# All four pairs of heads mixed in one step, values and plain-path loads taken two pairs at a time, in an attention + ELU + SiLU kernel

## The chip, the core and the metric

The kernel runs on one core of one Trainium2 chip. The metric is device time in microseconds (us) of one launch on that core; the lower the better. The median of the kernel before is 925.0 us, of three runs from 924.09 to 925.73 us. "p", "scores" and the like are named as in the code; TensorE is PE in the rows, VectorE DVE, ScalarE ACT, GpSimd POOL, SyncE SP.

## The reference

Causal attention with a window of 128 keys and a linear bias per head, then two feed-forward layers with weights of 512 x 2048 and 2048 x 512; everything is float32.

```python
def _attn_ref(q, k, v):                      # q, k, v: (4, 8, 576, 64)
    scores = scale * np.matmul(q, k.transpose(0, 1, 3, 2))
    mask = (rel >= 0) & (rel < window)       # rel: query position less key position, window 128
    scores = np.where(mask, scores + bias[None], -1000000000.0)
    scores = scores - np.max(scores, axis=-1, keepdims=True)
    attn = np.exp(scores)
    attn = attn / (np.sum(attn, axis=-1, keepdims=True) + 1e-09)
    return np.matmul(attn, v)

x = attn_out.transpose(0, 2, 1, 3).reshape(2304, 512)
h = x @ w_in
x = np.where(h > 0.0, h, np.exp(np.minimum(h, 0.0)) - 1.0) @ w_out
h = x @ w2_in
out = (h * (1.0 / (1.0 + np.exp(-h)))) @ w2_out
```

## The kernel before

The 2304 tokens are 18 groups of 128. **Attention** runs over 36 *units*: unit `u` is a pair of groups `t = u // 4` and a pair of heads `hp = u % 4`. In the loop over `u` these steps follow each other, each for a unit of its own age, and on every engine instructions run in the order in which the loop writes them (the schedule is by hand):

- `scores(u)`: PE computes the scores of both heads (`s`), DVE adds the bias and takes the row maxima (line 512, four instructions a unit), ACT takes the four exponentials (line 517). Units below `PLAIN` = 16 multiply plain float32 (line 495); later ones multiply operands split in a rounded upper part and a remainder (line 498).
- `invert(u - 1)`, `normal(u - 1)`: DVE inverts the sums (lines 520, 521), POOL scales p (line 560).
- `turn(u - 2)`: PE transposes p (line 536); `evict(0)` on DVE and `evict(1)` on ACT copy it to `ptt` in SBUF (lines 547, 549).
- `mix(u - 4)`, in units of even number: PE multiplies values and transposed p of two units, that is of two pairs of heads, into `a` (line 579), and `keep` on ACT writes the result to `store[0][block]` (line 585), the input x of the first layer. Values are loaded for one pair of heads at a time (`load_v`).

The first layer's work fills PE's time between those steps. Groups of tokens form five *blocks* (of 2, 4, 4, 4, 4 groups). When the last pair of a block's last groups has been mixed, the block's x is complete. Then `split_x(block, c)` splits each of the four 128-row chunks c of x in `xh` (ACT, line 227) and `xl` (DVE, line 228), and the block's pieces go to the list `fill`: for every slice of the hidden layer four pieces `c = 0..3` of three matmuls (`h`, line 244), later the pieces of the second product (`y`, line 302). `point(n)` takes pieces from the head of that list, for four token groups `n` of them, at three points of a unit, `PIECES = (2, 1, 2)`: two behind `scores(u)`, one behind `mix`, two at the end of the unit. `may` stops the list at its head while a piece's operands aren't known to have been written.

The first two pairs' chunks c = 0, 1 are split two units before chunks 2, 3, since the first `mix` of a group pair stands in unit 4t + 4 and the second in unit 4t + 6:

```python
keep = mix(u - 4)                      # u even
...
if o + 2 * P == blocks[bi][1] * P:     # the block's last groups
    split_x(bi, hp - 1)
    split_x(bi, hp)
```

SP issues nearly all loads. In attention it loads per unit the keys (`load_k`), the queries (`load_q`) and the values; ten slices of weights of the first layer are loaded in units 1 to 14 (`WSLOTS`), and go through POOL, ACT and DVE (`rescale`, `sign`, `join`, `part`: lines 142 to 167) before PE can use them. The last block and everything behind it, both layers, run after attention in `layers`: `h` and `y` matmuls without a break.

Of the kernel before, what the change touches and what calls it, by code (L numbers as in the profile page):

```python
# [42 lines left out]
def attention_elu_silu_kernel(  # L43
# [40 lines left out]
    LAG = 2  # L84
    NR = 4
    PLAIN = 16
    WSLOTS = [*range(1, 15), *range(26, 34)]
    PIECES = (2, 1, 2)
    BANKS = 3
    UNITS = [(t, hp) for t in range(NG // 2) for hp in range(NPAIR)]  # L90
# [238 lines left out]
    def attention():  # L329

        with ExitStack() as actx:
# [12 lines left out]

            kk = [const.tile([P, 2, 2, 3 * P], F32R, tag=f"k{hp}", name=f"k{hp}") for hp in range(NPAIR)]

            vv = [[const.tile([P, 2, P], F32, tag=f"v{hp}{i}", name=f"v{hp}{i}") for i in range(2)]
                  for hp in range(NPAIR)]
            raw_k, raw_q, qs, lows, lows_k = {}, {}, {}, {}, {}

            def first_col(g):
# [9 lines left out]
                for j in range(2):  # L361
                    eng.memset(qz[(1 - j) * D:(2 - j) * D, i, j, :], 0.0)

            def load_k(u, eng=nc.sync):
                if u < NU:
                    t, hp = UNITS[u]
                    c0 = first_col(2 * t)
                    if u < PLAIN:
                        eng.dma_start(kz[:, u % 4, c0:], k[hp * P:(hp + 1) * P, (2 * t - 1) * P + c0:2 * (t + 1) * P])
                        return  # L370
                    if t == PLAIN // NPAIR:
                        r = kw[:, u % 2, 0:6 * P].rearrange("p (j t) -> p j t", j=2)
# [9 lines left out]
            def load_q(u, eng=nc.sync):  # L382
                if u < NU:
                    t, hp = UNITS[u]
                    if u < PLAIN:
                        for j in range(2):
                            eng.dma_start(qz[j * D:(j + 1) * D, u % 4, j, :],
                                          q[hp * P + j * D:hp * P + (j + 1) * D, 2 * t * P:2 * (t + 1) * P])
                        return
                    raw_q[u] = r = r_p.tile([P, 2, 2 * P], F32, tag="kqr", name="qr")  # L390
                    for x in range(2):
                        eng.dma_start(
                            r[x * D:(x + 1) * D],
                            q[hp * P:(hp + 1) * P, 2 * t * P:2 * (t + 1) * P].rearrange("(j d) t -> d j t", d=D))

            def load_v(u):
                if u < NU:
                    t, hp = UNITS[u]
                    nc.sync.dma_start(
                        vv[hp][t % 2],  # L400
                        v[2 * t * P:2 * (t + 1) * P, hp * P:(hp + 1) * P].rearrange("(g p) d -> p g d", p=P))

            clear(0)
            load_q(0, nc.scalar)
            load_k(0)
# [5 lines left out]
            load_k(1)  # L411
            load_q(1)
            ident = const.tile([P, P], F32, tag="ident", name="ident")
            make_identity(nc, ident)
            ident16 = const.tile([P, P], BF16, tag="ident16", name="ident16")
# [105 lines left out]
                nc.vector.reciprocal(sums[u], sums[u])  # L521

            pts = {}

            def turn(u):
                t, hp = UNITS[u]
                pt = ps_.pop(u)
                ptt = pts[u] = pt_p.tile([P, 2, 4 * P], F32, tag="ptt", name="ptt")
                ev = []
                for j in range(2):  # L530
                    ps = ps_t.tile([P, 4 * P], F32, tag="t", name="pt")
                    parts = []
                    for e in range(2):
                        c0 = first_col(2 * t + e)
                        for c in range(c0, 2 * P, P):
                            nc.tensor.transpose(ps[:, 2 * P * e + c:2 * P * e + c + P], pt[:, j, e, c:c + P], ident)  # L536
                        if parts and c0 == 0:
# [12 lines left out]
                return evict  # L550
# [11 lines left out]
            def mix(u):  # L562

                t, hp = UNITS[u]
                bi, o = home[2 * t]
                ps = ps_a.tile([P, 2, 2 * P], F32, tag="a", name="a")
                c0 = first_col(2 * t)

                parts = [(2 * t, 1, 3), (2 * t + 1, 3, 4)]
# [4 lines left out]
                for i in range(2):  # L574
                    ptt = pts.pop(u + i)
                    for x, (g, a, b2) in enumerate(parts):
                        q0, q1 = (a // 2) * P, ((b2 + 1) // 2) * P
                        for j in range(2):
                            nc.tensor.matmul(ps[j * D:(j + 1) * D, i, q0:q1],  # L579
                                             vv[hp + i][(g // 2) % 2][:, g % 2, j * D:(j + 1) * D],  # L580
                                             ptt[:, j, a * P:b2 * P], start=(i == 0 and x == 0),
                                             stop=(i == 1 and x == len(parts) - 1), skip_group_check=True)

# [5 lines left out]

            fill, fresh, rest = [], [], []  # L590
            known = set()
            held = [0]

            def group(made, freeing, cost, ready):
# [43 lines left out]
            for u in range(NU + 3):  # L638
# [1 line left out]
                calls[0] += 1  # L640
                last = 2 * FIRST_F + (u >= 20) * NRAW
                if u in WSLOTS:
                    weight_step(min(u + 2, last), (4, 1), 1, last)
                pop()
                if u < NU:
                    scores(u)
                point(PIECES[0])
                low_q(u + 1)
                low_k(u + 1)
                while owed:  # L650
                    owed.pop(0)()
                if u in WSLOTS:
                    weight_step(min(u + 2, last), (2, 3), 1, last)
# [36 lines left out]
                if u < 2:  # L690
# [119 lines left out]
```

## Time and profile before

| | |
|---|---|
| median of three runs | 925.0 us (924.09 to 925.73) |
| the profiled execution, its own time | 923.84 us |
| its span, first to last instruction | 922.1 us |
| granted TensorE clock, mean | 1.000 |
| PE busy | 909.5 us, 99% |
| DVE, ACT, POOL busy | 571.2, 434.4, 229.4 us |
| DMA | 59.82 MB, mean 65 GB/s |

The profiled execution took 1.74 us more than its span, and lies 1.2 us below the median. PE is busy nearly all the time, so the time is PE's own work plus the moments in which it waits. DVE, ACT and POOL are far from full over the whole span, but not in the first 60 us.

### The profile page before, as it was taken

Reading aid. Unit: us, or ns where it says so; the run is one execution under the profiler, and the core shown is the slowest. Engines: PE = TensorE matmul, PEld = TensorE weight load, DVE = VectorE, ACT = ScalarE, POOL = GpSimd, SP = SyncE. Lnnn points to the kernel's source line nnn. Section 1 sums busy time; section 2 is a strip of 40 time slices with the busy share of each in tenths; the row PEclk is TensorE's granted clock in tenths of the full one; section 3 lists DMA queues with packets and bytes.
Section 4 is the critical chain, followed back from the end, with each engine's and each line's share of the span. In section 5 each row is a group of like instructions: output and inputs, shape, how many; then the busy total and the mean of one; then the engine's idle time right before and its main releaser. Section 6 shows DMA issues by size and latency. Waiting matters only on the chain.

```text
span 922.1 us, 13077 instructions
## 1 busy us (share of the span) xinstructions
PE 909.5 (99%) x4754; PEld 761.0 (83%) x4754; DVE 571.2 (62%) x1186; ACT 434.4 (47%) x959; POOL 229.4 (25%) x316
## 2 busy tenths in 40 slices
PE   7999999999999999999999999999999999999998
PEld 5878888887878888889888888888888888888887
DVE  7996878983778776576555546644366554444422
ACT  7786777764555435333343255543533342233311
POOL 5544455553444202220012023220221021000000
PEclk9999999999999999999999999999999999999999
DMA  8634336320242202210002012210221010000011
GB/s 250 206 99 109 97 107 176 94 68 6 90 134 91 69 1 70 69 46 1 1 13 79 23 46 71 73 41 24 68 69 47 1 46 1 34 35 23 23 46 45
DMA packets 50479, 59.82 MB, mean 65 GB/s; under 512 B 3952, under 2 KB 44144, under 8 KB 50416
## 3 DMA queue, kind: packets, MB, share of 16 engines
q1 hardware_dynamic: 50256, 58.87, 21.0%
q8 instruction: 37, 0.61, 0.3%
q14 instruction: 26, 0.21, 0.1%
q10 hardware_dynamic: 160, 0.13, 0.1%
HBM read 54.26 MB, written 4.72 MB: 64 GB/s over the span
## 4 chain that ended last, share of the span: by engine, by line
PE 89%; DVE 3%; issue 3%; POOL 2%; DMA 1%; ACT 1%; SPq 0%; POOLq 0%; DVEq 0%; ACTq 0%
PE y L302 40%; PE h L244 39%; PE a L579 3%; PE pt L536 3%; PE s L495 2%; PE s L498 2%; POOL wl L164 1%; POOL wraw L142 1%; DMA y<-in_k_dram 1%; DVE p L512 1%; DVE gl L272 0%; DMA v<-in_v_dram 0%; DMA wraw<-in_moe_w_in_dram 0%; DVE e L257 0%; DVE k L465 0%
## 5 line engine op out<-in xcount | busy, mean ns | idle before, releaser
L244 PE MATMUL h<-xh,wh 128*128 128x512 f32 (+1 forms) x640 | 238.5, 373 | 0.0
L244 PE MATMUL h<-xl,wh 128*128 128x512 f32 (+1 forms) x640 | 235.7, 368 | 0.6 <-DVE xl L228 0.6
L244 PE MATMUL h<-xh,wl 128*128 128x512 f32 (+1 forms) x640 | 235.7, 368 | 0.0
L164 POOL TENSOR_TENSOR wl<-wraw,wh 128x512 fp32r<-128x512 f32 x54 | 75.5, 1401 | 401.4 <-ACT wh L162 401.4
L272 DVE TENSOR_TENSOR gl<-e,gh 128x512 fp32r<-128x512 f32 (+1 forms) x158 | 106.0, 671 | 103.8 <-ACT gh L266 103.6
L251 ACT ACTIVATE e<-h 128x512 f32<-128x512 f32 (+1 forms) x160 | 88.1, 551 | 173.6 <-PE h L244 152.7
L266 ACT ACTIVATE gh<-e 128x512 fp32r<-128x512 f32 (+1 forms) x160 | 94.0, 588 | 106.6 <-DVE e L258 63.8
L244 PEld LDWEIGHTS h<-xh,wh 128*128 128x128 f32 x640 | 120.7, 189 | 20.4 <-issue 1.2
L244 PEld LDWEIGHTS h<-xh,wl 128*128 128x128 f32 x640 | 120.6, 188 | 20.3
L244 PEld LDWEIGHTS h<-xl,wh 128*128 128x128 f32 x640 | 120.7, 189 | 19.9 <-DVE xl L228 0.8
L302 PE MATMUL y<-gh,wh 128*128 128x512 f32 (+1 forms) x320 | 121.1, 379 | 0.0
L302 PE MATMUL y<-gl,wh 128*128 128x512 f32 (+1 forms) x320 | 118.3, 370 | 0.9 <-DVE gl L272 0.8
L302 PE MATMUL y<-gh,wl 128*128 128x512 f32 (+1 forms) x320 | 117.9, 368 | 0.0
L302 PE MATMUL y<-wl,gh 128*128 128x512 f32 (+1 forms) x294 | 113.1, 385 | 0.0
L302 PE MATMUL y<-wh,gh 128*128 128x512 f32 (+1 forms) x294 | 113.1, 385 | 0.0
L302 PE MATMUL y<-wh,gl 128*128 128x512 f32 (+1 forms) x294 | 113.1, 385 | 0.0
L560 POOL TENSOR_SCALAR p<-p,sm 128x256 f32<-128x256 f32 (+2 forms) x144 | 72.6, 521 | 98.8 <-DVE sm L521 52.6
L260 DVE TENSOR_TENSOR e<-h,e 128x512 f32<-128x512 f32 (+1 forms) x80 | 51.0, 638 | 60.4 <-ACT e L251 59.7
L162 ACT ACTIVATE wh<-wraw 128x512 fp32r<-128x512 f32 x58 | 38.5, 667 | 90.9 <-DVE wraw L154 66.7
L517 ACT ACTIVATE p<-p,neg 128x256 f32<-128x256 f32 (+2 forms) x144 | 68.9, 481 | 19.9 <-DVE neg L512 18.3
L302 PEld LDWEIGHTS y<-gl,wh 128*128 128x128 f32 x320 | 60.4, 189 | 11.3 <-DVE gl L272 2.2
L302 PEld LDWEIGHTS y<-gh,wh 128*128 128x128 f32 x320 | 60.3, 189 | 11.0 <-issue 1.0
(76 smaller groups left out, 1194.7 us busy)
## 6 DMA issues: line engine op xcount, KB each, us to landing
wraw<-in_moe_w_in_dram SPq DMA_DIRECT2D x30, 512.0 KB, 3.8
wraw<-in_moe_w_out_dram SPq DMA_DIRECT2D x28, 512.0 KB, 3.3
qr<-in_q_dram SPq DMA_DIRECT2D x40, 128.0 KB, 2.9
v<-in_v_dram SPq DMA_DIRECT2D x36, 128.0 KB, 2.6
out_dram<-x SPq DMA_DIRECT2D x17, 256.0 KB, 2.0
kr<-in_k_dram SPq DMA_DIRECT2D x32, 128.0 KB, 2.9
y<-in_k_dram SPq DMA_DIRECT2D x12, 192.0 KB, 3.7
y<-in_q_dram SPq DMA_DIRECT2D x30, 64.0 KB, 2.9
```

Of the source, the lines that this page charges most:

```text
L162: nc.scalar.activation(h, f32(top), AF.Copy)
L164: nc.gpsimd.tensor_tensor(lo, f32(top), f32(h), op=ALU.subtract)
L244: nc.tensor.matmul(tiles["ps"][:, 0:w], a[:, cs], b2[:, c, 0:w], start=(c == 0 and x == 0), stop=(c == NKC - 1 and x == 2))
L251: nc.scalar.activation(e[:, 0:w], tiles["ps"][:, 0:w], AF.Exp if layer == 0 else AF.Sigmoid)
L260: nc.vector.tensor_tensor(e[:, 0:w], ps[:, 0:w], e[:, 0:w], op=ALU.mult)
L266: nc.scalar.activation(gh[:, 0:w], tiles["e"][:, 0:w], AF.Copy)
L272: eng.tensor_tensor(gl[:, 0:w], tiles["e"][:, 0:w], f32(gh[:, 0:w]), op=ALU.subtract)
L302: nc.tensor.matmul(tiles["ps"][:, s], a[:, cs], b2[:, s], start=(f == f0 and x == 0), stop=(f == f1 - 1 and x == 2))
L517: nc.scalar.activation(dst, dst, AF.Exp, bias=m, scale=-1.0, accum_out=a)
L536: nc.tensor.transpose(ps[:, 2 * P * e + c:2 * P * e + c + P], pt[:, j, e, c:c + P], ident)
L560: nc.gpsimd.tensor_scalar(dst, dst, by, 1.0, op0=ALU.mult, op1=ALU.mult)
L579: nc.tensor.matmul(ps[j * D:(j + 1) * D, i, q0:q1], vv[hp + i][(g // 2) % 2][:, g % 2, j * D:(j + 1) * D], ptt[:, j, a * P:b2 * P], start= ...
```

## The change

In units with `u % 4 == 2` two mixes stand one behind the other, `mix(u - 6)` and `mix(u - 4)`, and units with `u % 4 == 0` have none; only the last group pair keeps the old places (units 36 and 38). So that transposed p of the first two pairs can wait longer, its `ptt` lies in places of `store` that are not in use yet (`homes`). The first of the two mixes takes a PSUM buffer of the transposes (`ps_t`). A block's x is then complete all at once: chunks 0 and 1 are split at the end of that unit, chunks 2 and 3 in the next unit behind `scores(u)`, and pieces c = 2, 3 may not be taken before that has been written. Values are loaded for two pairs of heads at a time; keys and queries of the plain units, from unit 2 on, as well. Weights are loaded one unit later than before, from unit 0 on, and wait one more unit until they are rescaled, so that `rescale`, `sign`, `join` and `part` of the ten slices stay in their units.

```diff
-    WSLOTS = [*range(1, 15), *range(26, 34)]
+    WSLOTS = [*range(15), *range(26, 34)]
...
-            def load_k(u, eng=nc.sync):
+            def load_k(u, eng=nc.sync, n=2):
...
-                        eng.dma_start(kz[:, u % 4, c0:], k[hp * P:(hp + 1) * P, (2 * t - 1) * P + c0:2 * (t + 1) * P])
+                        if u % n == 0:
+                            eng.dma_start(
+                                kz[:, u % 4:u % 4 + n, c0:],
+                                k[hp * P:(hp + n) * P, (2 * t - 1) * P + c0:2 * (t + 1) * P].rearrange("(h p) t -> p h t", p=P))
...
             def load_v(u):
-                if u < NU:
+                if 0 <= u < NU and u % 2 == 0:
                     t, hp = UNITS[u]
                     nc.sync.dma_start(
-                        vv[hp][t % 2],
-                        v[2 * t * P:2 * (t + 1) * P, hp * P:(hp + 1) * P].rearrange("(g p) d -> p g d", p=P))
+                        vv[hp // 2][t % 2],
+                        v[2 * t * P:2 * (t + 1) * P, hp * P:(hp + 2) * P].rearrange("(g p) d -> p g d", p=P))
...
-                ptt = pts[u] = pt_p.tile([P, 2, 4 * P], F32, tag="ptt", name="ptt")
+                if t < NG // 2 - 1 and hp < 2:
+
+                    ptt = homes[min(t, 4)][:, hp].rearrange("p (j t) -> p j t", j=2)
+                else:
+                    ptt = pt_p.tile([P, 2, 4 * P], F32, tag="ptt", name="ptt")
+                pts[u] = ptt
...
                 if u in WSLOTS:
-                    weight_step(min(u + 2, last), (4, 1), 1, last)
+                    weight_step(min(u + 1, last), (4, 1), 2, last)
                 pop()
                 if u < NU:
                     scores(u)
                 point(PIECES[0])
                 low_q(u + 1)
+                while later:
+                    bi = later.pop()
+                    split_x(bi, 2)
+                    split_x(bi, 3)
                 low_k(u + 1)
...
                 if u % 2 == 0 and u >= 4:
-                    keep = mix(u - 4)
+
+                    if u - 4 >= NU - NPAIR:
+                        keep = mix(u - 4, ps_a)
+                    elif u % NPAIR == 2:
+                        mix(u - 6, ps_t)()
+                        keep = mix(u - 4, ps_a)
                 point(PIECES[1])
-                load_v(u)
+                load_v(u - 2)
...
-                        split_x(bi, hp - 1)
-                        split_x(bi, hp)
+                        if t < NG // 2 - 1:
+                            split_x(bi, 0)
+                            split_x(bi, 1)
+                            later.append(bi)
+                        else:
+                            split_x(bi, hp - 1)
+                            split_x(bi, hp)
...
-                                made_ready += [group(hidden(bi, f), 1, n, lambda i, f=f: (0, 0, f) in known)] * NKC
+                                made_ready += [group(hidden(bi, f), 1, n, lambda i, f=f, bi=bi: (0, 0, f) in known and (i < 2 or bi not in later))] * NKC
```

On ACT, around the end of unit 22 and in unit 23 (x of block 2 is `x_78`, complete in unit 22), the order before is:

```order
L517 ACTIVATE p,sm<-p,neg 128x256 x4
L310 ACTIVATE y_82<-y 128x512
L585 ACTIVATE x_78<-a 128x2x256
L310 ACTIVATE y_82<-y 128x512
L549 ACTIVATE ptt<-pt 128x512
L227 ACTIVATE xh<-x_78 128x512 x2
L472 ACTIVATE qs<-qr 128x512
L517 ACTIVATE p,sm<-p,neg 128x256 x4
L310 ACTIVATE y_82<-y 128x512
L549 ACTIVATE ptt<-pt 128x512
```

and of the changed kernel at the same place:

```order
L523 ACTIVATE p,sm<-p,neg 128x256 x4
L310 ACTIVATE y_82<-y 128x512
L601 ACTIVATE x_78<-a 128x2x256 x2
L310 ACTIVATE y_82<-y 128x512
L562 ACTIVATE y_84<-pt 128x512
L227 ACTIVATE xh<-x_78 128x512 x2
L478 ACTIVATE qs<-qr 128x512
L523 ACTIVATE p,sm<-p,neg 128x256 x4
L227 ACTIVATE xh<-x_78 128x512 x2
L310 ACTIVATE y_82<-y 128x512
L562 ACTIVATE y_84<-pt 128x512
```

Before, the pair of `xh` here is that of chunks 2 and 3, with chunks 0 and 1 two units back; now it is that of chunks 0 and 1, and the pair of chunks 2 and 3 stands behind the four exponentials of unit 23. On DVE the two `xl` of chunks 2 and 3 move in the same way, behind the row maxima of unit 23 and `qs`.

PE's own order in unit 23 stays as it is: `scores(23)`, the fill pieces c = 0 and c = 1 (three rows `h` each), piece c = 2, then the transposes of unit 21; likewise in units 15 and 31.

On PE in unit 24, where a mix of two pairs stands between the fill pieces before (`a` rows), the order before is

```order
L244 MATMUL h<-xh,wl_572 128x512
L579 MATMUL a<-ptt,v_123 64x256 x2
L579 MATMUL a<-ptt,v_123 64x128 x2
L579 MATMUL a<-ptt,v_122 64x128 x2
L579 MATMUL a<-ptt,v_125 64x256 x2
L579 MATMUL a<-ptt,v_125 64x128 x2
L579 MATMUL a<-ptt,v_124 64x128 x2
L244 MATMUL h<-xh,wh_571 128x512
```

and now

```order
L244 MATMUL h<-xh,wl_341 128x512
L244 MATMUL h<-xh,wh_340 128x512
L244 MATMUL h<-xl,wh_340 128x512
L244 MATMUL h<-xh,wl_341 128x512
L549 MATMUL pt<-ident,p 128x128 x8
```

The `a` rows are gone from between the fill pieces; twice as many stand behind each other in unit 26. In the whole program eight such places are gone (units 4, 8, ..., 32), five of them (16 to 32) between fill pieces of 128 x 512.

## Rows read from the trace of the kernel before

**Rows 1.** The page: engines' busy time, and the chain that ended last by engine.

```profile
PE 909.5 (99%) x4754; PEld 761.0 (83%) x4754; DVE 571.2 (62%) x1186; ACT 434.4 (47%) x959; POOL 229.4 (25%) x316
...
PE 89%; DVE 3%; issue 3%; POOL 2%; DMA 1%; ACT 1%; SPq 0%; POOLq 0%; DVEq 0%; ACTq 0%
```

**Rows 2.** Busy time by stage: from:to, length, engines' busy us, clock, DMA.

```profile
0.00:20.00 20.00, 13.99 (x71) 10.33 (x72) 13.96 (x65) 13.84 (x47) 10.91 (x31) 1.00 0.83 240
20.00:40.00 20.00, 18.55 (x128) 15.27 (x128) 19.69 (x65) 17.73 (x54) 11.01 (x20) 1.00 0.80 244
40.00:60.00 20.00, 18.95 (x139) 15.23 (x136) 18.16 (x63) 14.93 (x44) 7.84 (x15) 1.00 0.35 93
...
80.00:220.00 140.00, 139.56 (x947) 115.70 (x946) 115.09 (x339) 96.53 (x272) 73.35 (x126) 1.00 0.36 100
```

**Rows 3.** Timeline of unit 23: start, duration, engine, line; in brackets idle before.

```profile
126.46 1.14 ACT L227 ACTIVATE xh<-x 128x512 fp32r<-128x512 f32 x2
127.08 1.12 PE L498 MATMUL s<-k,qs 128*128 128x256 f32 x8
127.11 1.71 DVE L228 TENSOR_TENSOR xl<-x,xh 128x512 fp32r<-128x512 f32 x2 [0.95 <-ACT xh L227]
...
129.42 0.39 PE L244 MATMUL h<-xh,wh 128*128 128x512 f32 x1
...
130.11 1.04 PE L536 MATMUL pt<-ident,p 128*128 128x128 f32 x8
...
131.15 0.19 ACT L517 ACTIVATION_READ_ACCUMULATOR p<-p,neg 128x1 f32 x1
```

**Rows 4.** Timeline of unit 31, in the same columns.

```profile
179.38 1.28 DVE L228 TENSOR_TENSOR xl<-x,xh 128x512 fp32r<-128x512 f32 x2
...
181.28 0.39 PE L244 MATMUL h<-xh,wh 128*128 128x512 f32 x1
...
181.97 1.04 PE L536 MATMUL pt<-ident,p 128*128 128x128 f32 x8
...
182.83 0.19 ACT L517 ACTIVATION_READ_ACCUMULATOR p<-p,neg 128x1 f32 x1
```

**Rows 5.** Timeline of unit 15.

```profile
79.93 0.39 PE L244 MATMUL h<-xh,wh 128*128 128x512 f32 x1
80.01 0.19 ACT L517 ACTIVATION_READ_ACCUMULATOR p<-p,neg 128x1 f32 x1
...
80.62 1.04 PE L536 MATMUL pt<-ident,p 128*128 128x128 f32 x8
```

**Rows 6.** Timeline of PE in unit 32: a mix between fill pieces.

```profile
186.35 0.39 PE L244 MATMUL h<-xh,wl 128*128 128x512 f32 x1
186.66 1.96 PE L579 MATMUL a<-ptt,v 128*64 128x256 f32 x24
188.55 0.50 PE L244 MATMUL h<-xh,wh 128*128 128x512 f32 x1
188.89 0.40 PE L244 MATMUL h<-xl,wh 128*128 128x512 f32 x1
```

**Rows 7.** Timeline of the first 18 us: PE, ACT and DVE.

```profile
3.50 6.88 PE L495 MATMUL s<-y,y 128*128 128x128 f32 x24 [3.50 <-DVE bias L431]
...
11.59 0.68 ACT L144 ACTIVATE wraw<-wraw 128x512 int32<-128x512 uint32 x1 [1.53 <-DMA wraw<-in_moe_w_in_dram]
...
12.01 1.48 PE L495 MATMUL s<-y,y 128*128 128x128 f32 x8
...
16.36 1.97 PE L495 MATMUL s<-y,y 128*128 128x256 f32 x8 [1.30 <-DMA y<-in_k_dram]
...
17.61 0.42 DVE L512 CUSTOM_DVE_ANT_0 p<-s,bias 128x256 f32<-128x256 f32 x1 [1.06 <-PE s L495]
```

**Rows 8.** Timeline of units 7 (two rows) and 12 (two rows).

```profile
33.67 1.06 DVE L167 TENSOR_TENSOR wl<-x,wh 128x512 fp32r<-128x512 f32 x1
34.65 0.18 ACT L517 ACTIVATION_READ_ACCUMULATOR p<-p,neg 128x1 f32 x1
...
60.39 2.00 PE L579 MATMUL a<-ptt,v 128*64 128x256 f32 x24
60.87 1.73 POOL L560 TENSOR_SCALAR p<-p,sm 128x256 f32<-128x256 f32 x4 [2.36 <-DVE sm L521]
```

More of the change, by code (lines that the diff above doesn't have):

```diff
@@ L345, in attention @@
             kk = [const.tile([P, 2, 2, 3 * P], F32R, tag=f"k{hp}", name=f"k{hp}") for hp in range(NPAIR)]
-            vv = [[const.tile([P, 2, P], F32, tag=f"v{hp}{i}", name=f"v{hp}{i}") for i in range(2)]
-                  for hp in range(NPAIR)]
+            vv = [[const.tile([P, 2, 2 * P], F32, tag=f"v{h2}{i}", name=f"v{h2}{i}") for i in range(2)]
+                  for h2 in range(NPAIR // 2)]
             raw_k, raw_q, qs, lows, lows_k = {}, {}, {}, {}, {}
@@ L380, in load_k, with load_q @@
                             k[hp * P:(hp + 1) * P, (2 * t - 1) * P + c0:2 * (t + 1) * P].rearrange("(j d) t -> d j t", d=D))
-            def load_q(u, eng=nc.sync):
+            def load_q(u, eng=nc.sync, n=2):
                 if u < NU:
@@ L385, in load_q @@
                     if u < PLAIN:
-                        for j in range(2):
-                            eng.dma_start(qz[j * D:(j + 1) * D, u % 4, j, :],
-                                          q[hp * P + j * D:hp * P + (j + 1) * D, 2 * t * P:2 * (t + 1) * P])
+                        if u % n == 0:
+                            src = q[hp * P:(hp + n) * P, 2 * t * P:2 * (t + 1) * P]
+                            src = src.rearrange("(h j d) t -> j d h t", j=2, d=D)
+                            for j in range(2):
+                                eng.dma_start(qz[j * D:(j + 1) * D, u % 4:u % 4 + n, j, :], src[j])
                         return
@@ L396, in load_v @@
             def load_v(u):
-                if u < NU:
+                if 0 <= u < NU and u % 2 == 0:
                     t, hp = UNITS[u]
                     nc.sync.dma_start(
-                        vv[hp][t % 2],
-                        v[2 * t * P:2 * (t + 1) * P, hp * P:(hp + 1) * P].rearrange("(g p) d -> p g d", p=P))
+                        vv[hp // 2][t % 2],
+                        v[2 * t * P:2 * (t + 1) * P, hp * P:(hp + 2) * P].rearrange("(g p) d -> p g d", p=P))
             clear(0)
-            load_q(0, nc.scalar)
-            load_k(0)
+            load_q(0, nc.scalar, 1)
+            load_k(0, n=1)
             warm = st_p.tile([P, 4], F32, tag="neg", name="warm")
@@ L410, in attention @@
             clear(1)
-            load_k(1)
-            load_q(1)
+            load_k(1, n=1)
+            load_q(1, n=1)
             ident = const.tile([P, P], F32, tag="ident", name="ident")
@@ L523, in attention @@
             pts = {}
+            homes = [store[a][bi].rearrange("p c t -> p (c t)").rearrange("p (i t) -> p i t", i=2)
+                     for a, bi in ((0, 2), (0, 2), (0, 2), (0, 4), (1, 3))]
             def turn(u):
@@ L560, in normal, with mix @@
                         nc.gpsimd.tensor_scalar(dst, dst, by, 1.0, op0=ALU.mult, op1=ALU.mult)
-            def mix(u):
+            def mix(u, pool):
                 t, hp = UNITS[u]
                 bi, o = home[2 * t]
-                ps = ps_a.tile([P, 2, 2 * P], F32, tag="a", name="a")
+                if pool is ps_t:
+                    ps = pool.tile([P, 4 * P], F32, tag="t", name="a").rearrange("p (i t) -> p i t", i=2)
+                else:
+                    ps = pool.tile([P, 2, 2 * P], F32, tag="a", name="a")
                 c0 = first_col(2 * t)
@@ L579, in mix @@
                             nc.tensor.matmul(ps[j * D:(j + 1) * D, i, q0:q1],
-                                             vv[hp + i][(g // 2) % 2][:, g % 2, j * D:(j + 1) * D],
+                                             vv[hp // 2][(g // 2) % 2][:, g % 2, i * P + j * D:i * P + (j + 1) * D],
                                              ptt[:, j, a * P:b2 * P], start=(i == 0 and x == 0),
@@ L591, in attention @@
             known = set()
+            later = []
             held = [0]
@@ L652, in attention @@
                 if u in WSLOTS:
-                    weight_step(min(u + 2, last), (2, 3), 1, last)
+                    weight_step(min(u + 1, last), (2, 3), 1, last)
                 pop()
@@ L681, in attention @@
                     if o + 2 * P == blocks[bi][1] * P:
-                        split_x(bi, hp - 1)
-                        split_x(bi, hp)
+                        if t < NG // 2 - 1:
+                            split_x(bi, 0)
+                            split_x(bi, 1)
+                            later.append(bi)
+                        else:
+                            split_x(bi, hp - 1)
+                            split_x(bi, hp)
                         if hp == NPAIR - 1 and bi < NB - 1:
```

## The prediction, made before the changed kernel ran

> **What bounds the kernel now.** I read the page first. PE is busy for 909.5 us of a span of 922.1, and the chain that ended last runs over PE for 89% of the span [rows 1]. So the time moves only with PE's own work and with its waits. Next the busy time by stage: from 80 to 220 us PE has 139.56 of 140 us, DVE 115.09 and ACT 96.53. In the first 60 us it is different: PE has 13.99, 18.55 and 18.95 of each 20 us, and DVE 19.69 in the second and 18.16 in the third [rows 2]. The reader is to see two regimes: up to about 60 us DVE is the bound, and PE has room; behind that PE is the bound, and each us that it waits is a us of the end. Then the timeline at the places that the change touches. A difference of under 0.2% (1.85 us) is what a measurement of this kernel can't tell from none.
>
> **The change part by part.** *The later split of chunks 2 and 3, units 15, 23, 31.* Before, both chunks have been split when the unit's fill begins. Now their `xh` stands on ACT behind the unit's four exponentials, while PE's piece c = 2 stands right behind c = 1. What PE must wait for can be put together from the rows. In unit 23 piece c = 2 starts at 129.42 and its three matmuls end with the start of the transposes at 130.11, that is 0.23 us a matmul. The exponentials end at 131.15 + 0.19 = 131.34. The `xh` of one chunk takes 0.6 us by the pair's 1.14 (they overlap a little), so it is there at 131.94; the `xl` of it on DVE takes 1.28 / 2 = 0.64 by the row in [rows 4] or 1.71 / 2 = 0.85 by that in [rows 3]. I take 0.7, since the longer one shares its place with other waiting: 132.65. Behind that PE needs two matmuls more (0.46), and is at the transposes at 133.1 instead of 130.11: **+3.0 us** [rows 3]. In unit 31 the same sum is 182.83 + 0.19 + 0.6 + 0.65 + 0.46 = 184.73 against 181.97: **+2.8** [rows 4]. In unit 15: 80.01 + 0.19 + 0.6 + 0.65 + 0.46 = 81.91 against 80.62: **+1.3**; it is smaller because plain scores take PE longer and piece c = 2 comes later [rows 5]. Queued behind the waiting matmul is everything of PE, and there is nothing in PE's stage from 80 us on to hide it: 7.1 us in all. What would shorten it: the exponentials wait for DVE's row maxima, and these for the two `xl` ahead of them (in unit 23 from 127.11 to 128.82, [rows 3]). The `xl` of chunks 0 and 1 take that same place now, so I leave it; in unit 31 DVE may be up to 1 us earlier, because the double mix ahead gives it time. The bounds of the three are 5.4 and 8.0 us.
>
> *The same split in unit 7* falls in DVE's stage. Its `wl` follows the maxima at once at 33.67 [rows 8]. Now two `xl` stand between, and wait until the last exponential (34.65 + 0.18 = 34.83) and an `xh` of 256 columns (some 0.35) are done: DVE idles from 33.7 to 35.2, **+1.5 us on DVE**. PE's wait there is covered by DVE's being late anyway.
>
> *Loads.* In the first 18 us ACT waits 1.53 us for the first weights with the exponentials of unit 2 behind it, and the scores of unit 4 wait 1.30 us for keys that queue behind three weights of 512 KB; DVE then idles 1.06 us for those scores [rows 7]. With one weight a unit, from unit 0 on, and pairs of keys and queries ahead of it, both waits should go. What DVE, the bound there, can win is its own idle time, **-1.1 us**. At least nothing is won; at most 2.8 (both waits in full). Later loads are halved in number and lie three units ahead, hidden behind PE; I cost them at nothing. SP is not waited for elsewhere. The later `load_v(u - 2)` comes four units ahead of its mix, hidden too.
>
> *The moved mixes.* A mix of two pairs costs PE its own work, which stays, and the change to and from its column halves, which is saved where the mix leaves the fill. In unit 32 the step into it is 0.31 us where a matmul takes 0.23, and behind it the first `h` takes 0.34 [rows 6]: 0.08 + 0.11 = 0.2 us that can be seen, and the last matmul's own exit is hidden in the merged row. I put that at as much as the entry, 0.3 in all. Five places between fill pieces lie in PE's stage: **-1.5 us** (at least 5 x 0.2 = 1.0, at most 8 x 0.3 = 2.4).
>
> But one moved mix loses its cover. In unit 12 the mix runs from 60.39 to 62.33 while the transposes behind it wait anyway for p, which POOL scales from 60.87 to 62.60, itself waiting 2.36 us for DVE [rows 8]. Taken out, PE idles there, and the 1.94 us of work come back in unit 14, which is already PE's stage. Against that stands DVE's chain: it leaves unit 13 at -1.1 (loads) + 1.5 (unit 7) - 1.3 (two `xl` that leave unit 12, 1.28 us by [rows 4]) = -0.9 us. PE reaches unit 15 at -0.9 + 1.9 = **+1.0 us** (from -1.0 with the start won in full, to +2.5 with nothing won).
>
> *Homes and the PSUM buffer* add no instruction. The second half of the transposes in units with two mixes waits for the first `keep` on ACT (0.6 us); the second mix and a fill piece (some 2.5 us on PE) lie between, which covers it.
>
> *Sum:* 7.1 + 1.0 - 1.5 = +6.6 us on the profiled execution's own 923.84 us (its span and 1.74 around it), 930.4. That execution lies 1.2 us below the median of the runs, so I forecast **931.5 us** for the median. With all terms at their lower ends 5.4 - 1.0 - 2.4 = +2.0, at their upper ends 8.0 + 2.5 - 1.0 = +9.5: 927.0 to 934.5.
>
> [...]
>
> **The rivals.** *The start gives back more (faster).* PE is idle for 6.0 + 1.45 + 1.05 = 8.5 us in the first 60 us [rows 2], 3.5 of them ahead of the first score [rows 7], so 5.0 us could be won if paired loads freed the whole start. With the splits at 5.4 and the mixes at 2.4: 925.0 + 5.4 - 2.4 - 5.0 = 923.0 us. It decides from a gain of 4.9 us on. Against it: DVE had 19.69 of 20 us from 20 to 40. Chance 0.09.
>
> *The splits come earlier than I think (no change).* If the double mix lets DVE start the maxima at once in units 23 and 31, as early as 0.7 us behind the start of the scores instead of 128.82 - 127.08 = 1.7 [rows 3], each stall shrinks by a us; with the start won too, 5.1 - 1.0 - 2.4 = +1.7 us: 926.5. Against it: DVE's `xl` are held there by ACT, not by DVE's own lag. Chance 0.11.
>
> *The clock falls in the stalls.* If PE, after each of the two long waits, ran for 6.9 us at the start's pace, it would lose 6.88 - 3 x 1.48 = 2.4 us each: 931.5 + 4.8 = 936.3. For it: the start; against it: no slow stretch behind 1.30 us of idle time. Chance 0.07. [...]
>
> *DVE becomes the bound in runs of three units without a mix.* DVE is busy for 82% of PE's stage [rows 2]; so far a mix in every second unit lets it catch up, now three units follow each other without one. If that costs a us in each of four such runs: 935.5. Over four units DVE has enough room, so I give it 0.08.
>
> **How the numbers follow.** My forecast has 0.65; the rivals 0.09, 0.11, 0.07, 0.08. Slower by over 0.2% (above 926.85): 0.65 + 0.07 + 0.08 = 0.80. Same: 0.11, and faster: 0.09. The range of 926.0 to 935.6 holds the forecast's own 927.0 to 934.5, the case of no change and that of DVE, and leaves out the faster case and the clock.
>
> **What would show it.** In the profile after: on PE a wait of an `h` matmul for ACT's `xh` and DVE's `xl` (lines 227, 228) some 2 to 3 us long in units 23 and 31, about 1 us in unit 15; waits for the first weights and for the keys of unit 4 gone; steps of about 0.3 us into a mix fewer by eight; scores of unit 15 at about 77.5 us instead of 76.47. I am wrong if PE doesn't wait for `xh` and `xl` there, or if those scores come 2 us or more before 76.47.

## The result and the profile after

The changed kernel takes 936.56 us (median of five runs, 933.45 to 937.34) against 925.0 us before (five runs, 924.09 to 925.73): a ratio of 1.0122, 95% interval 1.0111 to 1.0133. It is slower, as forecast, but by 11.6 us where 6.5 was forecast, and just outside the range. One of the five runs has a mean granted clock of 0.999 and took 933.45 us; the other four, at 0.994 to 0.996, took 936.40 to 937.34. The profiled execution took 936.56 us, with a span of 934.8; that of before took 923.84 with 922.1 [rows 1].

The page of the changed kernel: busy time, and the chain that ended last by engine.

```profile
PE 912.3 (98%) x4754; PEld 764.1 (82%) x4754; DVE 571.6 (61%) x1186; ACT 434.8 (47%) x959; POOL 227.0 (24%) x316
...
PE 87%; DVE 4%; ACT 3%; issue 3%; POOL 2%; DMA 1%; POOLq 0%; ACTq 0%; DVEq 0%
```

What PE waited for in the changed kernel (us in all, how often, the longest):

```profile
PE h L244 <- ACT xh L227: 7.0, 4, 2.3
PE s L501 <- DMA y<-in_q_dram: 3.6, 1, 3.6
PE pt L549 <- POOL p L573: 2.1, 3, 1.1
PE h L244 <- DVE e L258: 2.0, 1, 2.0
PE pt L549 <- ACT x L601: 1.9, 2, 1.2
PE h L244 <- DVE xl L228: 0.7, 3, 0.2
```

The waits for `xh` and `xl` are there, four of them where the forecast priced three. Two kinds were priced at nothing: the transposes' for line 601 (the writing out of the mixes from PSUM; 0.74 us in unit 6 and 1.17 in unit 10) and the `h` matmul's for DVE's `e`. The waits for the first weights and for unit 4's keys [rows 7] are gone. Busy time by stage, in the columns of [rows 2]:

```profile
0.00:20.00 20.00, 15.07 (x66) 11.23 (x66) 14.82 (x66) 14.48 (x49) 11.46 (x31) 1.00 0.87 254
20.00:40.00 20.00, 15.49 (x100) 12.49 (x99) 15.98 (x50) 14.69 (x42) 11.08 (x20) 0.91 0.78 246
40.00:60.00 20.00, 17.68 (x135) 15.20 (x133) 15.34 (x56) 11.27 (x35) 5.48 (x10) 0.91 0.16 46
...
120.00:140.00 20.00, 17.94 (x133) 14.94 (x131) 13.98 (x46) 15.53 (x48) 9.73 (x18) 1.00 0.33 96
...
180.00:200.00 20.00, 17.64 (x124) 13.89 (x123) 17.21 (x51) 13.10 (x37) 10.45 (x19) 1.00 0.33 95
```

From 20 to 40 us DVE fell from 19.69 to 15.98 us: it no longer sets the pace there, it starves. And the granted clock is 0.91. Unit 7's timeline, and the clock behind it in steps of 2 us, show both:

```profile
33.34 0.50 ACT L523 ACTIVATE p<-p,neg 128x256 f32<-128x256 f32 x1
33.83 0.71 ACT L227 ACTIVATE xh<-x 128x256 fp32r<-128x256 f32 x2
34.27 0.76 DVE L228 TENSOR_TENSOR xl<-x,xh 128x256 fp32r<-128x256 f32 x2 [1.56 <-ACT xh L227]
34.29 0.38 PE L244 MATMUL h<-xh,wh 128*128 128x256 f32 x1 [2.32 <-ACT xh L227]
...
40.59 0.42 DVE L518 CUSTOM_DVE_ANT_0 p<-s,bias 128x256 f32<-128x256 f32 x1 [2.75 <-PE s L501]
...
44.83 0.39 PE L244 MATMUL h<-xh,wh 128*128 128x256 f32 x1 [1.98 <-DVE e L258]
```

```profile
34.00:36.00 2.00, 1.63 (x11) 1.44 (x12) 1.73 (x4) 0.54 (x2) 0.00 (x0) 0.97 1.05 380
36.00:38.00 2.00, 2.00 (x11) 2.00 (x10) 1.76 (x5) 1.02 (x2) 0.55 (x2) 0.50 1.02 346
38.00:40.00 2.00, 2.00 (x12) 1.86 (x11) 0.00 (x0) 0.99 (x3) 1.91 (x4) 0.68 0.23 88
40.00:42.00 2.00, 2.00 (x15) 1.75 (x14) 1.28 (x9) 0.95 (x4) 0.00 (x0) 1.00 0.00 0
...
46.00:48.00 2.00, 2.00 (x13) 2.00 (x12) 1.32 (x3) 0.52 (x3) 2.00 (x4) 0.53 0.00 0
48.00:50.00 2.00, 2.00 (x8) 1.57 (x8) 0.42 (x1) 1.94 (x5) 0.07 (x1) 0.62 0.00 0
```

PE waits 2.32 us for unit 7's `xh`, then runs at a granted clock of 0.50 from 36 to 38 us and of 0.68 from 38 to 40. The scores of unit 8 come late, and DVE idles 2.75 us for them (the wait and the slow stretch both have a part in that). PE in turn waits 1.98 us for DVE's `e` in unit 8; behind that the clock is down again, 0.53 and 0.62 from 46 to 50 us, which is the second 0.91 above. In unit 23 the timeline is what the forecast put together from [rows 3]:

```profile
138.05 0.49 ACT L523 ACTIVATE p<-p,neg 128x256 f32<-128x256 f32 x1
138.45 0.18 ACT L523 ACTIVATION_READ_ACCUMULATOR p<-p,neg 128x1 f32 x1
138.55 1.13 ACT L227 ACTIVATE xh<-x 128x512 fp32r<-128x512 f32 x2
139.21 0.50 PE L244 MATMUL h<-xh,wh 128*128 128x512 f32 x1 [1.84 <-ACT xh L227]
139.94 0.50 PE L244 MATMUL h<-xl,wh 128*128 128x512 f32 x1 [0.22 <-DVE xl L228]
```

The start of a unit's scores on PE tells where the time went. I took it from the timelines of six kernels, at units where the same mixes have been done in all of them, so that the numbers can be compared. Each is the kernel's start less that of before, in us; the first scores of all start within 0.27 us of each other. The last four kernels are those of the experiments below. Each row is one profile. Kernels that have the same program up to unit 15 start it up to 0.9 us apart: at 75.54, 75.73, 76.08 and 76.46 us in the four profiles with the loads alone up to there, at 77.14, 77.70 and 77.76 in the three with unit 7 split at once.

```
unit                               11      15      19      23      31     end
before, start                   53.90   76.47  102.59  127.08  178.94  922.13
changed kernel                  +7.92   +7.64   +8.72   +7.79   +9.76  +12.63
loads alone                     -0.95   -0.93   -0.93   -0.96   -0.61   -0.74
all chunks split at once        +1.58   +1.29   +0.92   +0.01   -0.61   +1.74
block 0 at once, PE kept busy   +1.54   +1.23   +2.33   +1.40   +3.39   +6.44
all blocks late, PE kept busy   +4.46   +4.19   +5.27   +4.34   +6.34   +9.42
```

### The profile page after: what moved, and what is told of

It reads as the page before. It is cut to its first block, busy times and chain, and to the rows that moved or that the text cites. A ratio compares the mean times of both kernels' runs of the same rounds, so it can differ in the third digit from the quotient of the medians.

```text
span 934.8 us, 12991 instructions
## 1 busy us (share of the span) xinstructions
PE 912.3 (98%) x4754; PEld 764.1 (82%) x4754; DVE 571.6 (61%) x1186; ACT 434.8 (47%) x959; POOL 227.0 (24%) x316
## 4 chain that ended last, share of the span: by engine, by line
PE 87%; DVE 4%; ACT 3%; issue 3%; POOL 2%; DMA 1%; POOLq 0%; ACTq 0%; DVEq 0%
PE y L302 39%; PE h L244 39%; PE pt L549 3%; PE a L595 3%; PE s L504 2%; PE s L501 2%; POOL wl L164 1%; ACT p L523 1%; POOL wraw L142 1%; DVE xl L228 1%; DVE p L518 1%; ACT xh L227 1%; DVE wraw L154 0%; DMA wraw<-in_moe_w_in_dram 0%; DVE wraw L149 0%
## 5 line engine op out<-in xcount | busy, mean ns | idle before, releaser
L573 POOL TENSOR_SCALAR p<-p,sm 128x256 f32<-128x256 f32 (+2 forms) x144 | 69.0, 498 | 113.3 <-DVE sm L527 71.6
```

## The experiments

All are measured beside a run of the kernel before on the same chip, and ratios are to that (its medians were 924.2 to 925.0 us).

**All four chunks split at once, at the end of the block's last unit.**

```diff
-                            split_x(bi, 0)
-                            split_x(bi, 1)
-                            later.append(bi)
+                            for c in range(NKC):
+                                split_x(bi, c)
```

> The changed kernel, but all four chunks of a block are split at the end of the unit in which its x is complete, none in the next unit. Theory (the deferred split is the loss, the moved mixes and loads are not): PE's waits for ACT xh in units 7, 15, 23 and 31 (7.0 us in the profile) and the slow stretches of the clock behind them go; the scores of unit 15, now 7.6 us later than before, stand within 2 us of before, and the median falls from 936.6 to 923 to 927 us. Rival (the double mixes upset the first stage: PSUM buffers shared with the transposes, p late in units 6 and 10): the waits for xh go, but unit 15 stays 4 us or more late, and the median is 929 to 932 us.

925.52 us, ratio 1.0003 (0.9994 to 1.0011). The late split costs 11.0 us; the rest of the change is worth nothing that can be measured. But it is not nothing inside. By the table the double mixes alone cost 2.2 us at unit 15 (+1.29 against -0.93 with the loads alone; 0.7 to 2.2 by the profiles listed above it), and in unit 10 the rows say how:

```profile
49.02 0.68 DVE L560 COPY ptt<-pt 128x512 f32<-128x512 f32 x1
49.75 1.96 PE L595 MATMUL a<-x,v 128*64 128x256 f32 x24 [2.13 <-DVE ptt L560]
...
54.29 1.06 ACT L601 ACTIVATE x<-a 128x512 f32<-128x512 f32 x2
55.01 0.63 PE L549 MATMUL pt<-ident,p 128*128 128x128 f32 x4 [0.98 <-ACT x L601]
```

The first mix, `a<-x`, multiplies values of units 4 and 5, whose transposed p has long been in SBUF. It waits 2.13 us because its PSUM buffer is one of the transposes', and DVE copies unit 7's transposes out of that only at 49.02. Later the transposes wait 0.98 us for the same buffer, since ACT writes the mix out behind four exponentials. That loss to the loads alone shrinks from 2.22 us at unit 15 to 1.85, 0.97 and 0.00 at units 19, 23 and 31, and at the end it is back at 2.48. Behind unit 31 PE waits for DVE, which has four `xl` to do at the end of unit 30 where before it had two:

```profile
184.48 1.09 PE L504 MATMUL s<-k,qs 128*128 128x256 f32 x7 [0.21 <-DVE k L471]
190.37 1.09 PE L504 MATMUL s<-k,qs 128*128 128x256 f32 x7 [0.34 <-DVE k L471]
199.12 1.09 PE L595 MATMUL a<-y,v 128*64 128x256 f32 x12 [0.68 <-DVE ptt L560]
```

**Only block 0 split at once.**

```diff
-                            later.append(bi)
+                            if bi:
+                                later.append(bi)
+                            else:
+                                split_x(bi, 2)
+                                split_x(bi, 3)
```

> The changed kernel, but only block 0 (unit 7) has all four chunks split at once; units 15, 23 and 31 keep the deferred split. Theory: the wait of 2.32 us in unit 7, the slow clock behind it and the 1.98 us wait of unit 8 go, which is about 6 of the 12.6 us: about 930.5 us, and the waits of units 15, 23, 31 stay at 1.3, 2.7 and 3.0 us. Rival (the first stage is late for the double mixes): no more than 2.3 us are won: 934 us.

933.42 us, ratio 1.0087 (1.0070 to 1.0104): between the two, and nearer the rival's number, though it is the theory's mechanism that shows: unit 15 starts at 77.14 us, 7.0 earlier than in the changed kernel. With unit 7's wait its stretch of low clock is gone, and so is that of unit 8: the granted clock is 1.00 from 20 to 60 us. But now the clock fell behind the waits of units 23 and 31, to 0.50 from 134 to 136 us and from 188 to 190, where in the changed kernel's profile the same waits left it at 1.00. Unit 23 of this kernel, in steps of 2 us:

```profile
130.00:132.00 2.00, 0.42 (x2) 0.00 (x0) 1.23 (x5) 2.00 (x9) 0.00 (x0) 1.00 0.02 4
132.00:134.00 2.00, 1.52 (x5) 0.96 (x6) 1.76 (x3) 1.21 (x3) 0.00 (x0) 0.83 0.42 116
134.00:136.00 2.00, 2.00 (x10) 1.90 (x9) 1.08 (x4) 0.32 (x1) 1.38 (x4) 0.50 0.23 61
136.00:138.00 2.00, 2.00 (x12) 1.63 (x10) 0.00 (x0) 0.80 (x2) 1.67 (x4) 0.82 0.75 222
```

The wait is 1.84 us as in the changed kernel, to the digit, and the unit takes 9.51 us instead of 7.89 (127.92 to 137.43, against 134.87 to 142.76): 1.6 us for the stretch. Unit 31 takes 9.47 us instead of 8.29: 1.2 us.

**The loads alone**: the kernel before with the change's loads and weight timing, mixes and splits as they were. It was measured twice.

```diff
-    WSLOTS = [*range(1, 15), *range(26, 34)]
+    WSLOTS = [*range(15), *range(26, 34)]
...
-                    weight_step(min(u + 2, last), (4, 1), 1, last)
+                    weight_step(min(u + 1, last), (4, 1), 2, last)
```

(and `load_k`, `load_q`, `load_v` for two pairs of heads, as in the change)

> The kernel before with the change's loads alone: paired values, keys and queries, weights from unit 0 on; mixes and splits as before. Theory: the scores of unit 4 stand 2 us earlier, as in the changed kernel, and some of it is kept: 923 to 924.5 us, faster than before by 0.5 to 2 us. Rival (the start is bound by VectorE in units 5 to 12, which eats it): 925 us, no difference.

> The kernel before with the paired loads and the timing of the weights, once more, beside the others on the same chip: 923.0 to 923.6 us. Theory and rival agree on it; it is the base that the double mix for two group pairs has to beat.

923.27 us, ratio 0.9982 (0.9974 to 0.9990), and 923.75 us, 0.9987 (0.9978 to 0.9995). It is faster than both kernels, though by less than the 0.2% at which I called a difference measurable. In the first of its profiles the units start about 0.95 us earlier from unit 6 to 28, close to the predicted -1.1. But the wait for unit 4's keys, which was to be the source of that, is still there:

```profile
14.93 1.96 PE L500 MATMUL s<-y,y 128*128 128x256 f32 x8 [1.28 <-DMA y<-in_k_dram]
```

The wait for the first weights is down to 0.15 us, and DVE idles 0.40 us for those scores instead of 1.06. In the three other profiles with these loads unit 15 starts 0.74, 0.39 and 0.01 us earlier than before. So the loads gain something, 1.6 and 0.5 us in the two pairs of medians; how much, and by which wait, isn't shown. A part of it is the clock: 2 of these 24 runs have a mean granted clock under 0.999, and 29 of the 72 runs of the kernel before that stand beside the experiments. Between the runs at 0.999 and above the medians differ by 1.0 and 0.4 us.

**The changed kernel with the old loads** of keys, queries and weights (values stay paired).

> The changed kernel with single loads of keys and queries and the weights' loads as before; mixes, splits and paired values as changed. Theory (the loads help at the start, and are not what makes units 7 to 15 late): units 4 and 5 lose their 2 us, the rest stays, and the median is 936.5 to 939 us. Rival (loads of pairs, which need both units of a pair to be done, make the early units late): below 934 us.

937.8 us, ratio 1.0138 (1.0120 to 1.0156), 1.2 us above the changed kernel. The intervals of the two ratios overlap, so that the loads gain as much here isn't shown. In its profile the clock falls in units 8 and 23 (to 0.50 from 44 to 46 us and from 140 to 142), in the changed kernel's in units 7 and 8.

**PE kept busy in the waits**, in the changed kernel and in the one with only block 0 split at once. The matmuls take the PSUM buffer of the mixes, which is free there, and nobody reads what they write.

```diff
+                late = len(later)
                 while later:
...
+                if late:
+                    ps = ps_a.tile([P, 2, 2 * P], F32, tag="a", name="busy")
+                    some = cuts[min(cuts)]
+                    for i in range(5 if bi == 1 else 16):
+                        nc.tensor.matmul(ps[:, 0, :], ident16, some, start=True, stop=True)
                 point(PIECES[1])
```

> The changed kernel with 16 small matmuls of 128 x 256 (some 1.7 us) that nobody reads, in units 7, 23 and 31 where PE waits for xh and xl (5 of them in unit 15, where the wait is 0.7 us). The waits stay, PE does not idle in them. Theory (a wait of 2 us costs itself, and in some places a stretch at the lower clock of 1.2 to 1.6 us more, as unit 23 took 9.5 us with that stretch and 7.9 without): the fall behind unit 7 goes, that of unit 8 may stay, so 933.5 to 935.3 us and no granted clock under 0.9 behind units 7, 23 and 31. Rival (the clock has nothing to do with PE being idle there, or the stretch costs nothing): 936.5 us, or more.

> The kernel whose unit 7 splits all four chunks at once (933.4 us, with the clock falling behind the waits of units 23 and 31), with 16 small matmuls in the waits of units 23 and 31 and 5 in that of unit 15. Theory: both falls go, 933.4 - 2.8 = 930.6 us, and the granted clock is 1.00 from 120 to 200 us. Rival: 933.4 us, the clock falls all the same.

933.47 us, ratio 1.0095 (1.0081 to 1.0109), and 930.02 us, 1.0059 (1.0045 to 1.0073): 3.1 and 3.4 us less than the same kernels without these matmuls, which do nothing for the result. The granted clock is 1.00 in both in every 20 us up to 240. The first of the two lands on the time of the one run of the changed kernel with a mean clock of 0.999 (933.45 us). Units 7 and 8 of the first:

```profile
31.51 1.92 PE L689 MATMUL busy<-mid,ident 128*128 128x256 bf16 x16
33.98 0.39 PE L244 MATMUL h<-xh,wh 128*128 128x256 f32 x1 [0.55 <-ACT xh L227]
...
38.73 0.42 DVE L518 CUSTOM_DVE_ANT_0 p<-s,bias 128x256 f32<-128x256 f32 x1 [1.21 <-PE s L501]
...
42.97 0.39 PE L244 MATMUL h<-xh,wh 128*128 128x256 f32 x1 [1.98 <-DVE e L258]
```

The wait for `xh` is filled and the clock stays up. DVE still idles for the scores of unit 8, now 1.21 us. In unit 8 the wait of 1.98 us stands as before, so it is no consequence of the slow stretch, and this time no slow stretch follows it: the granted clock is 1.00 from 42 to 48 us. The two kernels differ in block 0 alone, by 2.96 us at unit 15: that is the late split of unit 7 without the clock.

**The double mix for group pairs 4 to 7 alone**, on the kernel with the loads alone. `twice` holds for the units of these pairs; their first two transposed p have a home, and their blocks are split all at once.

```diff
...
-                    keep = mix(u - 4)
+                    if not twice(u - 4):
+                        keep = mix(u - 4)
+                    elif u % NPAIR == 2:
+                        mix(u - 6, ps_t)()
+                        keep = mix(u - 4)
...
```

> The kernel before with the paired loads, and the double mix for group pairs 4 to 7 alone (units 22, 26, 30 and 34; steps into a mix gone in units 20, 24, 28 and 32), all four chunks split at once there. Theory (the double mix costs time in the first 60 us, where transposes and mixes wait for DVE and ACT, and saves its switches later): 923.3 - 4 x 0.2 to 0.3 = 922.1 to 922.6 us. Rival (three units without a mix make DVE late, as the waits of units 31 and 34 with all four chunks at once suggest): 923.5 to 924.8 us.

924.48 us, ratio 0.9991 (0.9983 to 1.0000). (Its values are loaded a step too early for one of the mixes that read them, so it multiplies other numbers; its instructions are those meant.) The rival holds: by the timeline it is 1.26 us ahead of the loads alone at unit 31 (allowing for 0.20 us that it starts later) and 0.91 behind at unit 35, with the three waits for `k` and `ptt` of the kernel above.

**The double mix for group pairs 4 and 5 alone** (`twice` holds for 4 and 5; block 3 is split in two units as before; from unit 18 on values are loaded two units later, as in the change).

> The kernel before with the paired loads, and the double mix for group pairs 4 and 5 alone (units 22 and 26), all four chunks of block 2 split at once in unit 22; block 3 is split in units 28 and 30 as before. Theory (the double mix itself saves its switches in PE's stage, and what it lost from unit 31 on was DVE late behind four chunks split in unit 30 and the double mix of unit 34): no waits of the scores for k in units 31 and 32 nor of a for ptt in unit 34, and 923.3 - 0.4 to 0.9 = 922.4 to 922.9 us. Rival (saving and waits cancel wherever the double mix stands): 923.3 us or more.

923.18 us, ratio 0.9983 (0.9974 to 0.9992), beside 923.75 for the loads alone, measured with it: over the theory's 922.4 to 922.9 and just under the rival's 923.3. The waits are gone. PE from 180 to 200 us, in the kernel with all chunks at once, and then in this one:

```profile
180.00:200.00 20.00, 18.68 (x109) 14.71 (x109) 18.46 (x54) 12.51 (x37) 9.75 (x18) 1.00 0.24 67
```

```profile
180.00:200.00 20.00, 20.00 (x137) 16.58 (x137) 17.96 (x55) 12.84 (x38) 12.72 (x23) 1.00 0.27 80
```

From unit 20 to unit 27 it gains 0.68 us on the loads alone, for two steps into a mix that are gone: 0.34 us each, where I took 0.3. As a whole the two versions can't be told apart; the three medians lie 0.5 to 1.6 us below those of the kernel before beside them.

**The late split alone**, on the kernel before: chunks 2 and 3 one unit later behind the scores, pieces c = 2, 3 held until then, mixes and loads as they were.

> The kernel before, its mixes and loads as they were, with chunks 2 and 3 split one unit later behind the scores and pieces c = 2, 3 held until then: the late split alone. Theory (the late split is the loss by itself): 7.1 us in units 15, 23 and 31 and 1 to 4 us in unit 7 and by the clock, 932 to 936 us. Rival (it costs only together with the double mix): under 928 us.

936.67 us (934.20 to 940.01), ratio 1.0132 (1.0112 to 1.0152), a little over the 932 to 936 expected. The loss doesn't need the double mix. Its PE waits:

```profile
PE h L244 <- ACT xh L227: 6.3, 4, 3.1
...
PE h L244 <- DVE xl L228: 0.7, 3, 0.2
```

**The first of the two mixes ahead of the scores**, and **the two buffers swapped**, both on the kernel with all chunks at once (the first in units 6, 10 and 14 alone).

```diff
+                if u % NPAIR == 2 and 4 <= u < PLAIN:
+                    mix(u - 6, ps_t)()
                 if u < NU:
                     scores(u)
...
```

```diff
-                        mix(u - 6, ps_t)()
-                        keep = mix(u - 4, ps_a)
+                        mix(u - 6, ps_a)()
+                        keep = mix(u - 4, ps_t)
```

> The changed kernel with all four chunks split at once (925.5 us), in units 6, 10 and 14 the first of the two mixes ahead of the unit's scores, so that ACT writes it out ahead of the exponentials and the PSUM buffer is free for the transposes. Theory (the shared PSUM buffer costs time in the first 60 us): the transposes' waits for line x of 0.74 and 0.98 us are gone and the time is 924 to 925 us. Rival (DVE is what sets the pace there, the waits only stand where another would): the waits are gone, but the time is 925.5 us or more, since DVE gets the scores 2 us later.

> The changed kernel with all four chunks split at once (925.5 us), in which the first of the two mixes takes its own PSUM buffer and the second the one of the transposes. In unit 10 the first mix waited 2.13 us for a buffer that DVE's copy of unit 7's transposed p freed at 49.70 us, and ACT wrote the other half of that p at 51.08. Theory A (the shared buffer is what costs): the first mix starts at once, and the time falls by 1.5 to 2 us, to 923.5 to 924 us. Theory B (DVE and ACT set the pace there, and a mix that is taken out of unit 8 leaves PE to wait for unit 7's transposed p whatever the buffer): the first mix starts at once, but the second waits 1.3 to 1.6 us, and the time falls by 0.4 to 0.7 us at most, to 924.8 to 925.5 us.

930.85 us, ratio 1.0064 (1.0050 to 1.0079), and 930.36 us, 1.0052 (1.0035 to 1.0070). Both are some 5 us slower than with the buffers as they were. The first has the sign of its rival (925.5 us or more), not the size; for the second neither theory holds. Moved ahead of the scores, the mix leaves the transposes without a wait for line 601, as both said, but in unit 10 it waits for DVE's copy just the same, now with the scores behind it:

```profile
50.08 3.68 PE L595 MATMUL a<-x,v 128*64 128x256 f32 x24 [5.00 <-DVE ptt L560]
```

With the buffers swapped the first mix starts at once and the second waits 0.23 us, but then the transposes wait 2.67 us for the buffer:

```profile
48.50 1.96 PE L595 MATMUL a<-x,v 128*64 128x256 f32 x24
50.69 2.46 PE L595 MATMUL a<-ptt,v 128*64 128x256 f32 x24 [0.23 <-DVE ptt L560]
...
54.79 0.20 ACT L523 ACTIVATION_READ_ACCUMULATOR p<-p,neg 128x1 f32 x1
55.19 1.07 ACT L601 ACTIVATE x<-a 128x512 f32<-128x512 f32 x2
...
56.41 0.91 PE L549 MATMUL pt<-ident,p 128*128 128x128 f32 x4 [2.67 <-ACT x L601]
```

In both the clock fell in the 20 us of these waits (0.83 and 0.92 from 40 to 60 us), so a part of the 5 us is the clock's: the one run of the second kernel with a mean granted clock of 1.000 took 927.63 us, 2.1 above the kernel with the buffers as they were. So PE waits at whichever of the shared buffer's two ends is left: it is tied to DVE's copy ahead of it and to ACT's behind it. That a buffer of its own would win the time back is not shown, since it was not tried.

## Why the prediction was wrong in size

*Right: the late split in PE's stage.* Units 15, 23 and 31 take 1.44, 2.60 and 3.00 us longer than before (84.11 to 91.95, 134.87 to 142.76 and 188.70 to 196.99, against 6.40, 5.29 and 5.29), where I said 1.3, 3.0 and 2.8: 7.0 in all, against 7.1. With nothing but the split changed back, 11.0 us are gone.

*Right: the switches, and in size the loads.* A switch took 0.34 us against 0.3. The loads gave -0.93 at unit 15 against -1.1, but by the other profiles and the wait that stayed, the agreement is in part luck. From unit 15 to the end +5.6 was forecast, and it was 12.63 - 7.64 = +5.0: the 7.0 less 2.05, where I took 1.5. Some 0.6 of the 2.05 is unit 19, in which PE before waited 0.45 us for DVE's `gl` and now doesn't; that I had not forecast.

*Wrong: the first 76 us*, +1.0 forecast and +7.6 measured at unit 15. The kernels split that up, each term being the difference of two rows of the table:

| | forecast, unit 15 | measured, unit 15 | measured, end |
|---|---|---|---|
| loads | -1.1 | -0.93 | -0.74 |
| double mixes (lost cover 1.9, two `xl` less -1.3; switches -1.5 behind unit 15) | +0.6 | +2.22 | +2.48 |
| late splits of units 15, 23, 31 (7.1 behind unit 15) | 0 | -0.06 | +4.70 |
| late split of unit 7 | +1.5 | +2.96 | +2.98 |
| clock | 0 | +3.45 | +3.21 |
| together | +1.0 | +7.64 | +12.63 |

The first two terms vary with the profile that is taken, from -0.93 to -0.01 and from 0.7 to 2.2. Of the clock's 3.45 us 0.30 stand already at unit 7's scores (29.37 us against 29.07), ahead of the wait. Three steps failed.

The first is "PE's wait there is covered by DVE's being late anyway". DVE idles 1.56 us in unit 7, as I said, but PE's wait isn't covered: the scores of unit 8 stand behind it on PE, and DVE, the bound there, idles for them too, 1.21 us where PE is kept busy and 2.75 with the slow stretch. With unit 7 split at once DVE waits for neither. 1.56 and 1.21 make 2.8. A wait on PE that makes the scores late is here a wait on DVE. I put 1.5, it was 2.96.

The second is the clock. I left its fall out of the sum and gave it 0.07, on the row of a wait of 1.30 us with no slow stretch behind, and priced it in units 23 and 31. That row was one run's: the 29 runs named above of the same kernel have a mean granted clock under 0.999 and took 924.8 to 928.4 us, the other 43 923.4 to 925.1; where it fell in them no trace shows. In the changed kernel the clock fell behind units 7 and 8 and cost 3.2 us at the end (12.63 less 9.42), 3.1 in the medians (936.56 less 933.47). That the clock is the cause, and not the wait, is shown by the matmuls that do nothing: with them it reads 1.00 from 34 to 38 us, without them 0.97 and 0.50. So here idle time on PE did, in some runs, cost a stretch behind it at a granted clock down to 0.50.

The third is "the second mix and a fill piece (some 2.5 us on PE) lie between, which covers it", for the PSUM buffer. I looked at one end of the buffer only, and there the cover was too short. In units 6 and 10 no fill piece follows the second mix (in unit 6 there is none yet), the `keep` on ACT stands behind four exponentials, and the transposes wait 0.74 and 1.17 us (0.74 and 0.98 with all chunks at once); at the other end the mix waits 2.13 us for DVE's copy there, and 0.34 in the changed kernel. I also looked for a mix without cover in unit 12 alone. How much of the 2.22 us is the buffer's and how much the cover's, the runs don't separate: each change to the buffer moved the wait instead of removing it. That cause stays open.

*The rivals.* The clock did fall, but in another place. That its 936.3 us lies close to the measured 936.56 is luck. Its 2.4 us a stall was taken from the first scores, 6.88 us for 24 matmuls against 1.48 for 8 [rows 7], and there the granted clock is 1.00; no run shows that loss behind the waits of units 23 and 31, and the two stretches measured there cost 1.6 and 1.2 us. It put 4.8 us in those units, where the profile's clock stayed at 1.00; 3.2 us came behind units 7 and 8 instead, and the rest from the other two steps. DVE late in runs of units without a mix is half right: it shows from unit 31 on in the kernel with all chunks at once (0.21, 0.34, 0.68 us), and vanishes where PE is late itself. From unit 32's scores to the end that kernel takes 739.9 us, the kernels with late splits in block 3 737.8 to 738.0. So the late splits of units 15, 23 and 31, 7.0 us in their places, cost only 6.44 - 1.74 = 4.7 us at the end against it. The start gave back no more than the forecast's 1.1 us: in no profile with the loads alone does unit 15 start more than 1.0 us early.

Two sums of the forecast are off without consequence: 930.4 and 1.2 make 931.6, and the case of no change comes to 926.7, not 926.5.

## What to carry to other kernels

Before a wait is called covered because another engine is late, follow what the waiting engine was to do next: if that feeds the late engine, the wait is paid there too. A buffer that two kinds of work share has two ends; look up on both sides who frees it, and what stands ahead of that in its queue. And a wait on TensorE is to be priced with a slow stretch that may stand behind it: here waits of 1.84 to 2.32 us had one in some places and some runs, and the two that were measured by themselves, in units 23 and 31, cost 1.6 and 1.2 us. A row of one run that shows no such stretch does not rule it out.

## What was not expected of the hardware

The clock's fall is not decided by the wait alone. Behind a wait of 1.84 us in unit 23 the granted clock stayed at 1.00 in one kernel and fell to 0.50 in another; behind 1.98 us in unit 8 it fell to 0.53 in the changed kernel, and stayed at 1.00 in the one whose earlier wait was filled. Even the wait of 1.30 us ahead of unit 4's scores, which left no slow stretch in [rows 7], had one in the profile of the late split alone (scores of unit 4 at 17.55 us). There PE had waited 0.92, 0.55 and 0.51 us just before, from 12.8 us on; in the run of [rows 7] it was 0.72 us in all:

```profile
16.00:18.00 2.00, 0.70 (x3) 0.49 (x3) 0.00 (x0) 2.00 (x10) 2.00 (x6) 0.61 0.99 261
18.00:20.00 2.00, 2.00 (x6) 1.54 (x6) 0.26 (x1) 1.18 (x3) 1.22 (x3) 0.50 0.95 292
```

The runs of that kernel follow the mean granted clock: 934.20 us at 0.998, 936.00 at 0.996, 936.67 and 937.64 at 0.994, 940.01 at 0.991. Why waits of one length end in either way, no run here shows.
